# Splitting the first loads over two DMA queues, with fewer weight loads and another work order, in a fused attention and feed-forward kernel

## The chip, the cores and the metric

The kernel runs on one core of a Trainium2 chip. The metric is the device time of one execution in microseconds; lower is better. The five engines of the core are TensorE (PE), VectorE (DVE), ScalarE (ACT), GpSimd (POOL) and SyncE (SP). SyncE, ScalarE and GpSimd can issue DMA transfers, each on a queue of its own.

## The reference

The input is one sequence of 2048 rows with 640 columns, all in bf16. It is normalised row by row, and two branches read the normalised rows `xn`:

```python
x = A_x
xn = _layernorm(x, axis=-1)
return x + _A_ref(xn, A_wqkv, A_wo) + _B_ref(xn, B_w1, B_b1, B_w2, B_b2)

# branch A: 32 heads of 20 columns, each row sees itself and the 7 rows
# at distances 2, 4, ..., 14 before it
off = jnp.arange(8) * 2
logits = einsum("bhsd,bhswd->bhsw", q, k[rows - off]) * 20 ** -0.5   # rows before 0: -1e9
o = einsum("bhsw,bhswd->bhsd", softmax(logits), v[rows - off])
A = o.reshape(B, S, 640) @ wo

# branch B: 640 -> 1536 -> 640
B = gelu(xn @ w1 + b1) @ w2 + b2
```

## The kernel before

The 2048 rows are cut into 16 blocks of 128 and four chunks of 512 rows (`NCH` = 4, `BPC` = 4 blocks each). The chunks are numbered `n` = 0 to 3, and everything runs with features on the partitions: `xnT` is the transposed normalised chunk.

Each chunk goes through the same steps. Statistics of its blocks: `st` on VectorE (two halves and an aggregation, L213 and L215) or, for chunks 2 and 3 and for block 1, sums and squares `su` and `sq` on ScalarE (L225, L232). Then the inverse deviation `rs` (logarithm and exponential on ScalarE, L244 and L247), the normalisation `xn` (L262, L264), and the transpose: on TensorE for chunk 0 (`tp`, L279, copied out by `tc`, L284), by DMA for the others (L291). Then the projections to q, k and v: for chunk 0 in small pieces (`ga`, `gb`, `gd`, `ge` for q of blocks 0 and 1, L346; `hj` for pairs of blocks, L377), for the others as groups of five 512-column matmuls (`pj`, L333), each copied out of PSUM by ScalarE (`gc`, `hc`, `pc`). The attention products of q with k are VectorE work (`qk`, L430), folded over the feature tiles (`pa`, L465, and `pb`, L471), summed per head by TensorE (`lg`, the logits, L480), then a softmax (`cp`, `m`, `mx`, `ex`, `ss`, `ri`, `at`). The weights of the softmax are spread over partitions by DMA (`xe`), multiplied with v (`av`, L581), and folded (`ac`, on VectorE or by an accumulating DMA, `ad`, `ot`). The feed-forward branch is `f1` (five matmuls, L611) and `ge` (gelu on ScalarE, L627). The output product takes w2 and wo: `t` for chunks 0 to 2 (three or five matmuls, L690), turned by `u`, `ut` and added to the output in memory by `ud`; `o` and `ohi` for the last chunk (L646), added to x by `dl` and `dh` (L658) and stored (L663). The output first receives x itself (`xp`, L300).

The order in which all these pieces are issued is written out by hand in `ORDER` (L40): each engine runs its own pieces strictly in that order and waits on semaphores for what others deliver. Ahead of the list stand the input loads, in the order of the queues, and a filling of matmuls on a constant: `WARM` of 512 columns and three of 128.

The first loads: SyncE issues block 0 of x, q's weights, blocks 2 and 3, k's weights, blocks 4 to 7, v's weights and w1 in two halves (L126, L129, L142). ScalarE issues block 1 and the two biases (L132 to L134). A small memset of block 1's first columns on GpSimd (L120) stands ahead of block 1's load. The biases land as rows in `b_rt`, are turned by one matmul `tb` (L453) and copied to `bT` by `b1` (L456). `ldx`, `ld2` and `ldo` issue the rest of x, w2 and wo on SyncE later (L148, L153, L157).

Of the kernel before, what the change touches and what calls it, by code (L numbers as in the profile page):

```python
# [45 lines left out]
pa01 su20 xp2 pj110 pc100 ld2 pj101 pc110 su22 pb01 pj104 su21 pj102 pc101 su23 pb04 pj114 pc104 ng2 pc102 pj112 ldo
sq22 sq21 lg0 pj111 cp0b cp0a pc112 pj113 mask m0b pc111 pc114 m0a xp1 hj211 pc113 mx0b xp0 mx0a hj210 qk13 ex0a pj122
ex0b hc210 pj123 sq23 ss0b t040 pc122 ss0a sq20 pj124 qk12 hc211 t000 rs2 pc123 f10_4 ri0a pc124 pj120 ri0b at0a rc2
qk11 f10_6 pj121 ge0_4 xn23 f10_7 xn21 qk10 tc23 t041 ge0_6 t001 tc21 pc121 su33 f10_8 pc120 at0b f11_9 su32 pa10 xe00
ge0_7 f11_1 xn20 f11_3 ge0_8 tc20 pa11 xn22 f11_10 ge1_1 tc22 ge1_9 t042 pb11 su31 xe03 t002 xe02 hj202 f10_9 xe01  # L50
hc202 ge1_10 pb14 su30 f10_10 ge0_9 pj203 ge0_10 lg1 pc203 pj210 cp1a av00 cp1b f11_5 ng3 sq32 f11_0 pc210 ge1_5 av01
pj202 ac00 ge1_0 hj212 pc202 pj212 sq30 m1 hc212 pj211 ac01 ge1_3 sq31 av03 t003 pad12 pj222 pc211 pc212 pad21 pj201
mx1 pj220 av02 ex1 t043 pc201 pj224 sq33 pj204 ss1 pc220 pc224 f12_6 pc222 ac03 ri1 pj223 at1 pj214 pc223 ac02 xe10
pc204 pj200 xe13 rs3 pc214 xe12 ad00 pad22 pj213 pc200 xe11 rc3 ad01 f11_6 pc213 xn33 pj221 ot00 xn30 tc33 ot01 f11_8
av10 t004 tc30 t044 u00 t010 av13 u04 ut00 t011 xn32 t012 xn31 tc32 t013 ud00 t014 av11 tc31 ac10 t030 u01 t031 pc221
t032 t033 ac13 ac11 t034 av12 f11_7 t020 t021 ge2_6 t022 ge1_6 ac12 t023 ge1_8 t024 u03 ut01 ad11 f12_9 ot11 pj303
ge2_9 qk22 f11_2 f11_4 ge1_2 pc303 pj301 qk23 ge1_4 f11_11 t130 ge1_11 t131 ad10 ge1_7 f12_2 u02 pc301 ut02 pa21 t140
pad31 ge2_2 pj300 ut03 pj311 ot10 ut04 ud01 f12_3 qk21 pc311 pc300 f13_2 ud02 pj312 xb qk20 pj314 pc312 ud03 pj302
pc314 ge2_3 pj313 pa20 pj304 t132 pc304 pb21 t133 pc302 t134 t141 u13 pb24 f13_5 pj310 ge3_5 ge3_2 lg2 t142 cp2a t143
cp2b t100 pc310 m2 pad32 f13_4 pc313 mx2 t101 qk30 f13_3 ex2 t144 f13_0 ss2 u14 f13_1 qk33 t102 ge3_3 ge3_1 t103 ge3_4  # L60
t110 f13_10 qk31 t104 ri2 f13_8 qk32 ge3_0 pj322 u10 f12_10 ge3_10 t111 at2 ge2_10 f12_8 pa31 pc322 xe22 ut10 f13_6
t112 pa30 f12_5 xe21 xe23 t113 ge2_5 xe20 t120 pb31 ge3_8 f12_0 ge3_6 ge2_8 t114 pb34 f12_4 u11 ut11 ud10 pj321 lg3
pj324 cp3b av21 ge2_4 t121 pc324 t122 cp3a pj323 m3 ac21 f12_7 pc323 mx3 ge2_0 t123 ge2_7 av20 o300 pc321 f13_9 f12_1
ex3 av23 ac20 f13_11 t124 ge2_1 pj320 ac23 u12 ge3_9 ut12 ud11 ud04 f13_7 pc320 ss3 ge3_11 t200 ge3_7 t230 av22 t231
f12_11 ri3 o301 at3 o302 ac22 xe33 ge2_11 t201 xe32 t202 xe31 ad21 t203 ut13 o320 ot21 t232 ad20 o310 o311 ut14 ot20
o312 av33 t204 t233 u20 t234 ut20 av32 t210 u23 ud12 xe30 t211 t212 t213 av31 t220 t221 t214 t222 ac31 u21 t223 t224
av30 t240 u22 ud13 ud20 ut21 ud14 t241 t242 t243 ac30 o330 t244 ac32 o321 u24 ud21 ut22 ad30 ud22 ut23 o331 ut24 o313
ot30 o322 ac33 o303 ud23 o304 ad31 o314 ud24 ot31 dh0 o323 dh1 dl1 o324 dl0 dd1 dd0 o332 dl2 o333 dh2 dd2 o334 ohi dl3
dlo dh3 dhi
# [4 lines left out]
def kernel(  # L74
# [47 lines left out]
    wqkv_v = A_wqkv.rearrange("(t p) n -> p t n", p=P)
    w1_v = B_w1.rearrange("(t p) n -> p t n", p=P)

    def load_x(b0, b1):
        nc.sync.dma_start(x_sb[:, b0:b1, :], x_nb[:, b0:b1, :])  # L126

    def load_w(s):
        nc.sync.dma_start(wqkv[s][:], wqkv_v[:, :, s * D : (s + 1) * D])  # L129
# [2 lines left out]
    nc.scalar.dma_start(x_sb[:, 1, :], x_nb[:, 1, :])  # L132
# [4 lines left out]
    load_w(1)
    load_x(BPC, 2 * BPC)
    load_w(2)
    for c in range(2):  # L140
# [1 line left out]
        nc.sync.dma_start(w1_sb[:, :, cs], w1_v[:, :, cs])  # L142
# [5 lines left out]

    def do_ld2():
        w2_v = B_w2.rearrange("(t p) n -> p t n", p=P)  # L150
        for c in range(4):
# [1 line left out]
            nc.sync.dma_start(w2_sb[:, ts, :], w2_v[:, ts, :])  # L153
# [286 lines left out]
    def do_warm(n, cols):  # L440

        for _ in range(n):
            nc.tensor.matmul(
                idle[:, 0:cols],
                lhsT=ones[:, 0:P],
                rhs=ones[:, 0:cols],
                start=True,
                stop=True,
            )
# [3 lines left out]
        nc.tensor.matmul(tiles["tb"][:, 0 : FT + KT], lhsT=b_rt[:], rhs=ident[:, 0 : FT + KT], start=True, stop=True)  # L453

    def do_b1():
        nc.vector.tensor_copy(bT[:], tiles["tb"][:, 0 : FT + KT])  # L456
# [394 lines left out]
```

## Time and profile before

| | us |
|---|---|
| median of 3 runs | 205.5 (205.43 to 206.93) |
| the profiled execution, device time | 205.49 |
| its span, first to last instruction | 203.3 |
| TensorE busy | 199.4 (98%) |
| VectorE busy | 185.8 (91%) |
| ScalarE busy | 129.7 (64%) |
| GpSimd busy | 29.5 (14%) |

All times in the views are microseconds from the start of the span. A row of the timeline gives start, length, engine, source line, operation, what is written from what, shapes and count, and in brackets how long the engine stood before and what released it. Rows with a `q` behind the engine (SPq, ACTq) are DMA issues by that engine. In the view by stretches each row gives, per engine, the busy time and in brackets the count of instructions, then the TensorE clock, the mean busy share of the DMA engines and the rate in GB/s.

### The profile page before, as it was taken

The page shows a single profiled execution, that of the slowest core. Times are in us where ns is not written, and L with a number is a line of the kernel's source. Part 1 is how long each engine was busy: PE and PEld are TensorE (multiplying, and loading weights), DVE is VectorE, ACT ScalarE, POOL GpSimd, SP SyncE. Part 2 cuts the span into 40 slices and gives each one's busy share as a digit, 9 for nine tenths or more (in the row PEclk, how much of TensorE's full clock was granted, in tenths as well). Part 3 has the DMA queues.
Part 4 walks back from the last instruction along what each step waited for, and adds up shares of the span by engine and source line. Part 5 has one row for each costly group of instructions (what it writes and reads, how often), then busy time and mean ns, then how long its engine had stood idle before and what let it go on. Part 6 is the DMA issues. An engine that isn't in the chain of part 4 may idle for free.

```text
span 203.3 us, 2874 instructions
## 1 busy us (share of the span) xinstructions
PE 199.4 (98%) x1100; PEld 105.0 (52%) x1100; DVE 185.8 (91%) x159; ACT 129.7 (64%) x237; POOL 29.5 (14%) x35
## 2 busy tenths in 40 slices
PE   8999999999999999999999999999999999999994
PEld 3899455654454555444444544444444445444552
DVE  2899999899997999999999996999979999999981
ACT  5689979999979897555545437697447990211100
POOL 3000000000000400024202500000202702253420
PEclk9999999999999999999999999999999999999999
DMA  6996399940673681849912890001863898895951
GB/s 204 390 395 208 77 355 336 348 148 3 91 155 89 110 148 22 219 92 163 193 17 52 102 99 5 3 0 15 170 98 69 153 118 147 111 120 90 103 90 64
DMA packets 38430, 27.31 MB, mean 134 GB/s; under 512 B 25106, under 2 KB 34578, under 8 KB 38418
## 3 DMA queue, kind: packets, MB, share of 16 engines
q1 hardware_dynamic: 28016, 20.29, 38.2%
q0 software_dynamic: 10080, 6.56, 26.3%
q10 hardware_dynamic: 322, 0.30, 0.4%
q8 instruction: 8, 0.13, 0.3%
q14 instruction: 4, 0.03, 0.0%
HBM read 10.49 MB, written 4.59 MB: 74 GB/s over the span
## 4 chain that ended last, share of the span: by engine, by line
PE 96%; DMA 2%; SPq 0%; DVE 0%; issue 0%
PE T L690 27%; PE hps L611 25%; PE pps L333 24%; PE lo L646 7%; PE gps L377 7%; DMA wq_sb<-in_A_wqkv_dram 2%; PE hi L646 2%; PE gps L346 1%; PE L L480 1%; PE tp L279 0%; SPq L126 0%; DVE prod L658 0%; PE tb L453 0%
## 5 line engine op out<-in xcount | busy, mean ns | idle before, releaser
L611 PE MATMUL hps<-xnT,w_sb 128*128 128x512 bf16 x240 | 56.9, 379 | 0.0
L430 DVE TENSOR_TENSOR prod<-qT,kT 128x5120 bf16<-128x5120 bf16 x16 | 44.5, 2820 | 0.1
L690 PE MATMUL T<-hT,w_sb 128*128 128x512 bf16 x180 | 43.4, 379 | 0.0
L611 PEld LDWEIGHTS <-w_sb 128*128 128x128 bf16 x240 | 23.5, 98 | 27.5
L702 POOL DMA_DIRECT2D out_dram<-x_sb x15 | 20.9, 1492 | 87.5 <-DMA x_sb<-x_sb 87.5
L627 ACT ACTIVATE hT<-hps,bT 128x512 bf16<-128x512 f32 x36 | 23.9, 689 | 12.1 <-PE hps L611 9.6
L690 PEld LDWEIGHTS <-w_sb 128*128 128x128 bf16 x180 | 17.5, 98 | 21.1 <-issue 0.4
L693 ACT ACTIVATE x_sb<-T,bT 128x512 bf16<-128x512 f32 x15 | 10.3, 688 | 25.6 <-PE T L690 24.5
L581 DVE TENSOR_TENSOR prod<-vT,ax 128x5120 bf16<-128x5120 bf16 x8 | 22.4, 2820 | 2.7 <-PE L L480 1.5
L581 DVE TENSOR_TENSOR prod<-vT,x_sb 128x5120 bf16<-128x5120 bf16 x8 | 22.2, 2817 | 0.0
L592 POOL DMA_DIRECT2D prod<-prod x6 | 7.8, 1300 | 77.5 <-DVE prod L581 77.5
L170 ACT ACT_TABLE_LOAD x14 | 18.0, 1283 | 1.0 <-PEq L835 0.7
L471 DVE TENSOR_TENSOR prod<-prod 128x4096 bf16<-128x4096 bf16 x8 | 18.3, 2291 | 0.3
L333 PE MATMUL pps<-xnT,wv_sb 128*128 128x512 bf16 x75 | 18.5, 379 | 0.0
L690 PE MATMUL T<-oT,wo 128*128 128x512 bf16 x75 | 18.5, 379 | 0.0
L333 PE MATMUL pps<-xnT,wq_sb 128*128 128x512 bf16 x75 | 18.1, 379 | 0.0
L465 DVE TENSOR_TENSOR prod<-prod 128x4096 bf16<-128x4096 bf16 x8 | 18.0, 2286 | 0.0
L333 PE MATMUL pps<-xnT,wk_sb 128*128 128x512 bf16 x75 | 18.0, 380 | 0.0
L594 DVE TENSOR_TENSOR prod<-prod 128x2560 bf16<-128x2560 bf16 x10 | 14.8, 1487 | 0.1
L333 PEld LDWEIGHTS <-wq_sb 128*128 128x128 bf16 x75 | 8.8, 117 | 7.5
L333 PEld LDWEIGHTS <-wv_sb 128*128 128x128 bf16 x75 | 8.7, 118 | 7.6 <-issue 0.4
L333 PEld LDWEIGHTS <-wk_sb 128*128 128x128 bf16 x75 | 8.6, 118 | 7.7 <-issue 0.8
(91 smaller groups left out, 242.6 us busy)
## 6 DMA issues: line engine op xcount, KB each, us to landing
prod<-prod POOLq DMA_DIRECT2D x6, 640.0 KB, 6.8
ax<-attn SPq DMA_DIRECT2D x8, 256.0 KB, 3.9
x_sb<-attn SPq DMA_DIRECT2D x8, 256.0 KB, 4.5
w_sb<-in_B_w_dram SPq DMA_DIRECT2D x2, 960.0 KB, 11.0
out_dram<-x_sb SPq DMA_DIRECT2D x3, 640.0 KB, 6.8
w_sb<-in_B_w_dram SPq DMA_DIRECT2D x4, 480.0 KB, 6.6
out_dram<-x_sb POOLq DMA_DIRECT2D x15, 128.0 KB, 5.6
x_sb<-in_A_x_dram SPq DMA_DIRECT2D x2, 640.0 KB, 7.0
```

Source lines behind the costliest of these rows:

```text
L170: nc.scalar.preload_act_table_set(name)
L333: nc.tensor.matmul(ps[:], lhsT=wqkv_p[which][:, ti, to, :], rhs=xnT[:, ti, :], start=(ti == 0), stop=(ti == KT - 1),)
L430: nc.vector.tensor_tensor(out=prod[:, j], in0=q[:, :, at].unsqueeze(1).to_broadcast([P, W, KT, P]), in1=window(k, at), op=ALU.mult,)
L465: nc.vector.tensor_tensor(out=low, in0=low, in1=high, op=ALU.add)
L471: nc.vector.tensor_tensor(out=first, in0=first, in1=rows[:, :, t * P : (t + 1) * P], op=ALU.add)
L581: nc.vector.tensor_tensor(out=prod[:, j], in0=window(qkv_tile(n, 2), slice(j * P, (j + 1) * P)), in1=ax_view(n)[:, j, :, :].unsqueeze(2).t ...
L594: nc.vector.tensor_tensor(out=low, in0=low, in1=high, op=ALU.add)
L611: nc.tensor.matmul(ps[:], lhsT=w1_sb[:, ti, ft * P : (ft + 1) * P], rhs=tiles["xnT", n][:, ti, :], start=(ti == 0), stop=(ti == KT - 1),)
L627: nc.scalar.activation(hT, tiles["hps", n, ft][:], ACT.Gelu_apprx_tanh, bias=bT[:, ft : ft + 1], scale=1.0)
L646: nc.tensor.matmul(out_ps(bl, hi), lhsT=lhs, rhs=rhs[:, CH:D] if hi else rhs[:, 0:CH], start=pc == 0 and k == 0, stop=pc == 4 and k == len ...
L690: nc.tensor.matmul(ps[:], lhsT=lhs, rhs=rhs, start=pc == 0 and k == 0, stop=pc == 4 and k == len(srcs) - 1)
L702: nc.gpsimd.dma_start(dst, src, accum_op=ALU.add)
```

## The change

- Blocks 0 and 1 of x are each loaded as two halves of 64 partitions, the first half on SyncE's queue and the second on ScalarE's. q's weights are loaded in two parts as well: feature tiles 0 to 2 by SyncE, 3 and 4 by ScalarE. The memset ahead of block 1 is gone.
- The biases are loaded by SyncE, behind v's weights and ahead of w1. `bT` is copied by ScalarE and no longer by VectorE.
- w1 is one load instead of two, w2 three instead of four, wo two instead of three.
- The filling has 9 long matmuls instead of 10.
- `ORDER` is another permutation of the same pieces.

```diff
-WARM = 10
+WARM = 9
...
-    nc.gpsimd.memset(x_sb[:, 1, 0:16], 0.0)
...
-    load_x(0, 1)
-    nc.scalar.dma_start(x_sb[:, 1, :], x_nb[:, 1, :])
-    nc.scalar.dma_start(b_rt[0:FT, :], B_b1.rearrange("(t p) -> t p", p=P))
-    nc.scalar.dma_start(b_rt[FT : FT + KT, :], B_b2.rearrange("(t p) -> t p", p=P))
-    load_w(0)
+    for b in range(2):
+        for queue, ps in ((nc.sync, slice(0, P // 2)), (nc.scalar, slice(P // 2, P))):
+            queue.dma_start(x_sb[ps, b, :], x_nb[ps, b, :])
+    for queue, a, b in ((nc.sync, 0, 3), (nc.scalar, 3, KT)):
+        queue.dma_start(wqkv[0][:, a:b, :], wqkv_v[:, a:b, 0:D])
     load_x(2, BPC)
     load_w(1)
     load_x(BPC, 2 * BPC)
     load_w(2)
-    for c in range(2):
-        cs = slice(c * F // 2, (c + 1) * F // 2)
-        nc.sync.dma_start(w1_sb[:, :, cs], w1_v[:, :, cs])
+    nc.sync.dma_start(b_rt[0:FT, :], B_b1.rearrange("(t p) -> t p", p=P))
+    nc.sync.dma_start(b_rt[FT : FT + KT, :], B_b2.rearrange("(t p) -> t p", p=P))
+    nc.sync.dma_start(w1_sb[:], w1_v)
...
-        for c in range(4):
-            ts = slice(c * FT // 4, (c + 1) * FT // 4)
+        for c in range(3):
+            ts = slice(c * FT // 3, (c + 1) * FT // 3)
             nc.sync.dma_start(w2_sb[:, ts, :], w2_v[:, ts, :])
...
-        for a, b in COLS:
+        for a, b in ((0, 3), (3, KT)):
             nc.sync.dma_start(wo2[:, a:b], A_wo.rearrange("(p t) n -> p t n", t=KT)[:, a:b])
...
-        nc.vector.tensor_copy(bT[:], tiles["tb"][:, 0 : FT + KT])
+        nc.scalar.copy(bT[:], tiles["tb"][:, 0 : FT + KT])
```

The two orders begin like this (of 626 names each):

```diff
-pad01 pad02 st00a st00 sum1 rs00 neg1 xn00a sq1 xn00b tp00a wa tp00b tc00a wb rs01 tc00b ga xn01b gb2 xn01a tp01b
-st03a tp01a tb tc01b gb3 tc01a gb4 st03 gd gc0 st02a ge rs03 st02 hj101 xn03 rs02 gc1 xn02 tp03 gc4 st12a tp02 tc03
+pad02 pad01 st00a st00 sum1 rs00 neg1 xn00a sq1 wa xn00b tp00a ho tp00b tc00a wb ga tc00b rs01 gb2 xn01a xn01b tp01a
+gb3 st03a tp01b tc01a gb4 st02a tc01b gd st02 gc0 ge st03 rs02 hj101 xn02 rs03 gc1 xn03 tp02 gc4 tp03 st10a hj100 tc03
```

Further differences that the prediction speaks of: `ho`, the reduce that makes `head_of` (L190), moves from behind the statistics of chunk 1 to between `tp00a` and `tp00b`; `tb` and `b1` move to behind k's and q's pieces of chunk 0; `xp1` takes the place of `xp2` behind `ldx`, ahead of `ld2`; on VectorE `qk32` moves ahead of `m2`; around the fourth logits `lg3` three `f1` groups (`f12_0`, `f12_8`, `f13_0`) move behind it and `t121`, `t122`, `t123` ahead of it.

More of the change, by code (lines that the diff above doesn't have):

```diff
@@ L46 @@
[L46 to L69, printed above, removed]
+pad02 pad01 st00a st00 sum1 rs00 neg1 xn00a sq1 wa xn00b tp00a ho tp00b tc00a wb ga tc00b rs01 gb2 xn01a xn01b tp01a
+gb3 st03a tp01b tc01a gb4 st02a tc01b gd st02 gc0 ge st03 rs02 hj101 xn02 rs03 gc1 xn03 tp02 gc4 tp03 st10a hj100 tc03
@@ new lines @@
+sq23 hj202 ss0a pj120 hc202 pc121 ss0b ri0a hj211 sq20 qk10 hj210 pc120 ri0b pc122 pj123 rs2 hc210 f10_4 rc2 qk12 xn21
+f10_9 hc211 tc21 pc123 f10_8 qk11 f10_6 ge0_4 xn22 f10_10 ge0_9 tc22 t041 ge0_10 pa11 f11_1 pad21 ge0_6 xn20 f10_7
+ge0_8 pa10 tc20 f11_10 xn23 ge0_7 t001 tc23 su33 f11_3 at0a at0b ge1_10 pb11 xe00 t002 ge1_1 xe03 f11_9 xe02 pj124
+ge1_9 pb14 xp2 su32 hj212 pc124 pj203 xe01 ge1_3 su31 lg1 pj213 su30 av00 cp1a f11_0 hc212 ng3 pc203 pj210 sq32 av02
+pad12 pj214 ac00 ge1_0 pc210 pj201 cp1b pc213 pc214 f11_5 av01 sq30 t042 ge1_5 pj211 sq31 t043 sq33 m1 ac01 pj212 mx1
@@ new lines @@
+pj224 av03 rs3 pc201 t003 pc212 pj221 ex1 pj204 pc211 ss1 pj202 pc204 ac02 ri1 pj200 pc202 pc221 at1 pj223 rc3 ac03
+xe11 xn30 pj220 xe12 pc200 xe10 ad00 pc224 f11_8 xn33 xe13 pj222 pc223 ad01 pc220 tc30 f11_4 ot00 f11_6 ot01 av11 t004
+tc33 t044 u00 pc222 t010 u04 ut00 av12 ac11 t011 xn31 t020 xn32 tc31 t021 t022 av10 t023 tc32 t012 t013 f11_7 av13
+ac10 t014 t024 ud00 u01 pad31 t030 ac13 t031 ge1_6 t032 ac12 ge1_4 t033 t034 ad11 f11_2 u03 ut01 ge1_7 ot11 f12_2
+ge1_2 qk23 f11_11 ge2_2 pad22 f12_6 ge1_11 ge1_8 f12_3 qk22 ge2_6 pj314 pj303 ad10 t130 pc303 pj300 ot10 pj312 pc300
@@ new lines @@
+pa21 pc314 t131 u02 pj313 ge2_3 ut02 pc312 qk21 f13_5 pc313 ut03 t132 ut04 ud01 pj311 qk20 pj304 pc311 ud02 t140 pc304
+pj301 ud03 pa20 pj302 xb pj310 pc302 pb21 t133 f13_2 t134 ge3_2 pb24 pc310 f12_9 ge3_5 pc301 t141 u13 lg2 f12_4 cp2a
+qk32 cp2b t100 ge2_9 pj322 t142 m2 f13_1 mx2 t101 qk33 ex2 t143 t102 t144 ge2_4 qk31 f13_8 ge3_1 f13_4 ge3_8 u14 f13_6
+pc322 ss2 t120 f12_5 qk30 ri2 f13_10 t121 ge2_5 t122 at2 ge3_4 t103 pa31 ge3_10 xe21 f13_3 xe22 xe20 t104 ge3_3 pa30
+pj321 u10 ut10 t110 t111 pb31 t112 xe23 t113 t114 pb34 f12_10 u11 ut11 ud10 t123 lg3 f12_1 av20 t124 ge2_1 cp3a pj320
@@ new lines @@
+pc321 cp3b av21 f12_7 ac20 ge2_10 ge3_6 f12_11 u12 pad32 pc320 ut12 pj324 ge2_7 av23 ac21 f13_0 ud11 f12_0 ge3_0
+ge2_11 ud04 m3 f13_9 ge2_0 mx3 pj323 ac23 f12_8 ex3 t230 ss3 o300 ge3_9 t231 av22 ge2_8 t200 t201 t232 ri3 f13_7 at3
+o301 ac22 xe30 ge3_7 t202 xe31 pc323 t233 xe33 ad20 pc324 t203 ut13 o310 ot20 o311 ad21 f13_11 ot21 ut14 o312 av30
+t204 t234 u20 ut20 t210 u23 ud12 ac30 t211 xe32 t212 av31 t213 t220 t221 t222 t214 av33 t223 u21 t224 t240 ac31 u22
+ud13 ud20 ut21 ud14 t241 ge3_11 t242 ad30 t243 o302 ac33 t244 av32 o320 u24 ud21 ut22 o303 ud22 ut23 ut24 o321 o322
@@ L70 @@
+ac32 o330 o331 ot30 ud23 o313 ad31 o323 ud24 o304 ot31 o314 dh0 dl0 dd0 o324 dl1 dh1 dd1 o332 dh2 dl2 o333 dd2 o334
+ohi dl3 dlo dh3 dhi
 """.split()
```

8 lines of the change are left out of this document (5 added, 3 removed).

## The prediction

> **What bounds the kernel now.** I read the page first, then the chain of work that ended last in order of time, then the waits, then the first 36 us instruction by instruction.
>
> ```profile
> span 203.3 us, 2874 instructions
> ...
> PE 199.4 (98%) x1100; PEld 105.0 (52%) x1100; DVE 185.8 (91%) x159; ACT 129.7 (64%) x237; POOL 29.5 (14%) x35
> ...
> PE 96%; DMA 2%; SPq 0%; DVE 0%; issue 0%
> ```
>
> The chain of work in order of time (start, length, what):
>
> ```profile
> 1.19 5.07 DMA wq_sb<-in_A_wqkv_dram
> 6.31 1.03 PE gps L346 x15
> ...
> 9.64 1.09 PE gps L377 x10
> 10.73 0.56 PE tp L279 x10
> ...
> 43.05 0.65 PE T L690 x3
> ...
> 45.42 1.08 PE hps L611 x5
> ...
> 200.62 0.29 DVE prod L658
> ```
>
> From 6.31 to 200.6 us the chain is TensorE and nothing else: a group of five 512-column matmuls costs 1.08 us and a group of three 0.65 us wherever it stands, so 194.3 us of the span is matmul work laid end to end. The change neither removes nor adds any matmul behind 6.31. A new order can therefore only keep this stretch or put holes in it; a gain must come from ahead of 6.31, and it must survive the next meeting of TensorE with another engine. So I looked at the front, engine by engine:
>
> ```profile
> 0.74 0.39 SPq L126 DMA_DIRECT2D x_sb<-in_A_x_dram  x1
> ...
> 0.88 0.38 ACTq L132 DMA_DIRECT2D x_sb<-in_A_x_dram  x1
> ...
> 3.27 0.89 DVE L213 BATCH_NORM_STATS2 stats<-x_sb 128x6 f32<-128x320 bf16 x2 [3.27 <-DMA x_sb<-in_A_x_dram]
> ...
> 3.65 0.74 ACT L225 ACTIVATE trash<-x_sb 128x640 bf16<-128x640 bf16 x1 [1.63 <-DMA x_sb<-in_A_x_dram]
> ...
> 4.50 0.29 ACT L244 ACTIVATE logv<-mv,eps_t 128x1 f32<-128x1 f32 x1
> ```
>
> ```profile
> PEld L346 <- DMA wq_sb<-in_A_wqkv_dram: 0.3, 1, 0.3
> ```
>
> Block 0 lands at 3.27, block 1 at 3.65, q's weights at 6.3. The first q matmul needs the first copy of block 0's transpose and the weights; the weights come last, and TensorE stands 0.3 us for them. Next, the meeting at the first logits (L480):
>
> ```profile
> 10.88 1.28 DVE L213 BATCH_NORM_STATS2 stats<-x_sb 128x6 f32<-128x320 bf16 x3 [0.22 <-DMA x_sb<-in_A_x_dram]
> ...
> 14.90 0.23 DVE L190 TENSOR_REDUCE head_of<-ident 128x32 bf16<-128x128 bf16 x1
> 15.05 0.17 DVE L456 COPY bT<-tb 128x17 f32<-128x17 f32 x1
> ...
> 15.66 11.03 DVE L430 TENSOR_TENSOR prod<-qT,kT 128x5120 bf16<-128x5120 bf16 x4
> ...
> 31.13 4.62 DVE L471 TENSOR_TENSOR prod<-prod 128x4096 bf16<-128x4096 bf16 x2
> ```
>
> ```profile
> 33.44 2.32 PE L333 MATMUL pps<-xnT,wk_sb 128*128 128x512 bf16 x10
> 35.80 0.62 PE L480 MATMUL L<-prod,head_of 128*32 128x512 bf16 x8
> ```
>
> VectorE's last fold ends at 31.13 + 4.62 = 35.75 and the logits start at 35.80. TensorE was through with its ten matmuls at 33.44 + 2 x 1.08 = 35.60, so it already stands some 0.1 to 0.2 us for VectorE. And VectorE has no gap from 15.66 to 35.75; that run begins where it does because blocks 4 to 7 of x landed at 10.88. Whoever wants the end earlier must bring those blocks earlier as well as TensorE's start.
>
> **The change part by part.**
>
> *Blocks 0 and 1 and q's weights over two queues.* The bytes in front of blocks 4 to 7 stay the same, but for the 4 KB of biases. What can be won is fill of the DMA engines:
>
> ```profile
> 2.50:3.00 0.50, 0.50 (x3) 0.22 (x2) 0.00 (x0) 0.00 (x0) 0.00 (x0) 1.00 1.08 359
> 3.00:3.50 0.50, 0.50 (x3) 0.17 (x2) 0.23 (x1) 0.00 (x0) 0.00 (x0) 1.00 0.93 261
> 3.50:4.00 0.50, 0.50 (x2) 0.15 (x1) 0.50 (x2) 0.35 (x1) 0.00 (x0) 1.00 0.88 318
> ...
> 4.50:5.00 0.50, 0.50 (x5) 0.28 (x3) 0.00 (x0) 0.47 (x3) 0.00 (x0) 1.00 1.08 397
> ```
>
> The last column is GB/s. Between 3.0 and 4.0 it is 261 and 318 against 397 later: (397 - 261) x 0.5 + (397 - 318) x 0.5 = 107 KB not moved, or 0.27 us at 397 GB/s. That is the most that a second queue can win for everything loaded behind it. The loss from the other side: each queue now issues two loads, not one, ahead of q's weights, and SyncE's issues stand 0.45 us apart (0.74 and 1.19), so the weights may start 0.45 us later. I take a gain of 0.13 us, half of the most, since both halves of the weights then have a queue that is already running. The trace has no split load, hence the bounds +0.27 and -0.45.
>
> The chain from block 0 to the first q matmul: the logarithm at 4.50 stands behind block 1's sum on ScalarE (3.65 + 0.74 and 0.19 more to read it), so block 0 alone being earlier brings nothing; block 1 has to be earlier too. The two blocks are the same bytes as before on the same two queues, and ScalarE's first issue no longer waits for the small memset (0.88 back to 0.74): 0 to 0.14 us. The weights' wait of 0.3 us bounds it too. TensorE's start moves by 0 to -0.3 us; I take -0.13 as well.
>
> [...]
>
> *The reduce of `head_of` moves from 14.90 to between the two normalisations and the first transposed copy.* It takes 0.23 us where VectorE waits for the transposes anyway, so I charge 0.05 us; without that cover 0.23. At 14.90 it hid, as did the bias copy (0.17, now on ScalarE), behind ScalarE's step for the inverse deviations: VectorE was through at 15.05 + 0.17 = 15.22 and its next large product began at 15.66. So their removal there gives nothing.
>
> *Biases behind v's weights.*
>
> ```profile
> wv_sb<-in_A_wqkv_dram SPq DMA_DIRECT2D x1, 800.0 KB, 9.3
> ```
>
> ```profile
> 3.65 0.85 SPq L129 DMA_DIRECT2D wv_sb<-in_A_wqkv_dram  x1
> ```
>
> v's weights land at 3.65 + 9.3 = 12.95, and the biases right behind. The matmul that turns them now stands behind five pieces of 1.09, one of 0.55 and ten transposes of 0.56 after the first k piece at 9.5, so at about 16.0: cover of 3 us. Behind it on TensorE stand all later matmuls, so lateness would be paid in full. Cost 0.
>
> *w1 in one load.* Its second half went out at about 6.7 and landed 12.0 us later, at 18.7:
>
> ```profile
> L142 SPq DMA_DIRECT2D w_sb<-in_B_w_dram x2: 368/1092/1816, 6.3 to 6.7; - x2
> ...
> DMA to landing us min/median/max: 6.3/8.5/12.0
> ```
>
> The first feed-forward matmul is at 20.5, and now needs all of w1: cover of 1.8 us, cost 0. w2 in three loads and wo in two save issues on SyncE, and the store of x that stands before them now copies blocks 4 to 7, long landed, and no longer blocks of the load just issued.
>
> ```profile
> 28.27 3.12 SPq L153 DMA_DIRECT2D w_sb<-in_B_w_dram  x4
> ```
>
> ```profile
> w_sb<-in_B_w_dram SPq DMA_DIRECT2D x4, 480.0 KB, 6.6
> ```
>
> The last of w2 was issued by 31.4 and landed some 6.6 us later, at 38.0. Its first use, 43 now, comes behind the first logits and four groups of five: 35.80 + 0.62 + 4 x 1.08 = 40.7. Even the old issue times leave 2.7 us. Cost 0.
>
> *One warm-up matmul fewer.*
>
> ```profile
> 0.78 4.43 PE L443 MATMUL idle<-const-bfloat16-1.0 128*128 128x512 bf16 x13 [0.78 <-PEq L835]
> ```
>
> ```profile
> 2.01 0.15 PEld L443 LDWEIGHTS <-const-bfloat16-1.0 128*128 128x128 bf16 x1 [0.28 <-issue]
> 2.44 0.15 PEld L443 LDWEIGHTS <-const-bfloat16-1.0 128*128 128x128 bf16 x1 [0.28 <-issue]
> ...
> 4.57 0.46 PEld L443 LDWEIGHTS <-const-bfloat16-1.0 128*128 128x128 bf16 x3 [0.28 <-issue]
> ```
>
> They start 0.43 us apart, twice the 0.216 us of later ones; from 4.57 on three loads fit in 0.46 us, so full speed comes some 3.9 us after the start. Nine of 0.43 and three short ones end at about 4.9, just past it. TensorE does nothing useful then: 0 us, with a rival below.
>
> *The other order.* I added up TensorE's groups ahead of each meeting in both orders. Ahead of the first and the third logits stand the very same pieces; ahead of the second one group of three is replaced by five short matmuls (0.1 us earlier). Ahead of the fourth, three groups of five give way to three groups of three: 3 x (1.08 - 0.65) = 1.3 us earlier. There VectorE's slack was less:
>
> ```profile
> 144.84 4.62 DVE L471 TENSOR_TENSOR prod<-prod 128x4096 bf16<-128x4096 bf16 x2
> ```
>
> ```profile
> 150.29 0.62 PE L480 MATMUL L<-prod,head_of 128*32 128x512 bf16 x8
> ```
>
> ```profile
> 125.73 0.43 DVE L524 TENSOR_TENSOR attn<-e 128x512 bf16<-128x512 bf16 x1 [1.82 <-ACT e L517]
> ```
>
> 150.29 - 149.46 = 0.83, so TensorE would stand 0.5 us. But VectorE's wait of 1.82 us at 125.7 is now filled by a product of q and k (`qk32` ahead of `m2`), and the fold ends up to 1.8 us earlier. Net cost 0, and 0.5 if that product's inputs are late. The last two meetings (the output's last five-tile sums) stand behind the same pieces on both engines. The tail is the same.
>
> **The sum.** 205.49 (the profiled execution, whose span is 203.3; 2.2 lie around it, and the median of the runs is 205.50) - 0.13 = 205.36, with the bounds of the split from 205.49 - 0.27 - 0.1 (TensorE's stand at the logits) = 205.1 to 205.49 + 0.45 = 205.9. **Forecast 205.4 us: no change that can be told apart.**
>
> **The rivals.**
>
> *The halves come late* (slower). ScalarE's queue carries half of block 0, and what it issued at 0.88 landed 0.38 us after SyncE's load. If each block waits for that queue and q's weights start a whole issue later, blocks 4 to 7 and TensorE's start both move by 0.45: 205.9. For it: the two landings; against it: that load was a whole block, not a half.
>
> *The split moves nothing*: the engines are shared, both orders hold, 205.5. For it: 1.08 of DMA share already at 2.5 us.
>
> *The clock is released late* (slower than before). Nine warm-ups end 0.2 us past the release seen here. If a release later than about 4.9 is missed and the count starts again with the transposes near 5.3, full speed comes at 5.3 + 3.9 = 9.2, and the q matmuls from 6.3 on run at half: (9.2 - 6.3) / 2 = 1.45, so 206.9. It decides from the point where the release falls behind the filling. Against it: the fast executions agree. [...]
>
> *A hole in the new order* (slower). One VectorE product, 11.03 / 4 = 2.8 us, ahead of its turn at a meeting without slack would be paid in full: 205.4 + 2.8 = 208.2. For it: TensorE has no slack anywhere; against it: the sums above.
>
> **How the numbers follow.** Forecast 0.62, halves late 0.15, nothing moves 0.10, late clock 0.07, hole 0.06. A measurement of this kernel tells about 1% (2.05 us) from no change. Only the hole goes beyond that: slower 0.06. No case gains 2 us, since the whole wait for the weights is 0.3: faster 0.01. The rest, 0.93, is the same. The range reaches from 205.0, under the best bound, to 207.0, over the late clock.
>
> **What would show it.** Right: the first q matmul at 6.1 to 6.3, VectorE's statistics of block 4 at 10.7 to 10.9, the first logits at 35.6 to 35.8, the last matmul near 200.5, and no TensorE wait over 0.3 us between. Wrong: q's weights after 6.5, half-speed rows behind 6.3, TensorE waiting at the fourth logits, or the bias matmul waiting for its load.

## The result and the profile after

| | before | after |
|---|---|---|
| median of the runs, us | 205.48 (205.22 to 208.37, 9 runs) | 207.18 (206.32 to 208.0, 9 runs) |
| ratio | | 1.0077, interval 1.0049 to 1.0104 |
| profiled execution, us | 205.49 | 206.32 |
| its span, us | 203.3 | 204.2 |

Here and below, medians and ranges count every run, while ratios and their 95% intervals leave out the few executions over 1.5% slower than the fastest of their kernel. The changed kernel is slower by 1.7 us in the median and by 0.8 us in its profiled execution, which is the fastest of its nine. The interval lies clear of 1, although the change is smaller than the 1% that the prediction took for the least that can be told. So there are two things to find: what every execution pays, and what most of the others pay on top. The head of the page of after and the shares of its chain:

```profile
PE 199.3 (98%) x1099; PEld 105.0 (51%) x1099; DVE 185.8 (91%) x158; ACT 129.1 (63%) x238; POOL 29.4 (14%) x34
...
PE 81%; DVE 12%; DMA 4%; SPq 1%; issue 0%; ACT 0%
```

TensorE has the same 199 us of work. But the chain, 96% TensorE before, now holds 12% VectorE and 4% DMA. In order of time (start, length, what) it begins like this:

```profile
0.74 0.60 SPq L132
...
1.40 0.80 SPq L132
...
2.25 0.61 SPq L134
...
2.91 0.49 SPq L125
...
3.95 7.77 DMA x_sb<-in_A_x_dram
...
16.62 10.94 DVE prod L430 x4
27.56 4.41 DVE prod L465 x2
...
34.32 2.30 DVE prod L471
...
36.67 0.61 PE L L480 x8
```

This is the changed place itself: SyncE's issues of the two halves (0.60 and 0.80 us) and of q's part (0.61) push the issue of blocks 4 to 7 to 3.95; they land at 11.72; from there to 36.62 the chain is VectorE, but for half a microsecond of ScalarE's inverse deviations, and the first logits wait for it. The timeline of after has the times to set beside those of the prediction:

```profile
0.74 1.47 SPq L132 DMA_DIRECT2D x_sb<-in_A_x_dram  x2
0.74 1.20 ACTq L132 DMA_DIRECT2D x_sb<-in_A_x_dram  x2
1.97 0.60 ACTq L134 DMA_DIRECT2D wq_sb<-in_A_wqkv_dram  x1
...
3.36 0.89 DVE L213 BATCH_NORM_STATS2 stats<-x_sb 128x6 f32<-128x320 bf16 x2 [3.36 <-DMA x_sb<-in_A_x_dram]
...
4.69 0.74 ACT L225 ACTIVATE trash<-x_sb 128x640 bf16<-128x640 bf16 x1 [0.80 <-DMA x_sb<-in_A_x_dram]
...
6.37 0.63 PE L279 MATMUL tp<-ident,xn 128*128 128x128 bf16 x5 [1.17 <-DVE xn L264]
...
7.05 1.00 PE L346 MATMUL gps<-xnT,wq_sb 128*128 128x128 bf16 x15
...
11.74 1.67 DVE L213 BATCH_NORM_STATS2 stats<-x_sb 128x6 f32<-128x320 bf16 x4 [0.24 <-DMA x_sb<-in_A_x_dram]
...
36.67 0.61 PE L480 MATMUL L<-prod,head_of 128*32 128x512 bf16 x8 [0.18 <-DVE prod L471]
```

Block 0 is there at 3.36 (3.27 before), block 1 at 4.69 (3.65), the first q matmul at 7.05 (6.31), blocks 4 to 7 at 11.74 (10.88), the first logits at 36.67 (35.80). TensorE stands 1.17 us between the filling and the first transposes. The first logits are 0.87 us later and the last long stretch of the output product 0.85 us (198.11 against 197.26), which is the whole difference of the spans (204.2 against 203.3, each rounded to a tenth). TensorE itself was ready for the logits at 36.67 - 0.18 = 36.49, 0.69 us later than they began before. So both ways to the logits became late, and VectorE's a little more.

Where the 0.86 us of the loads went is in the view by stretches, the first 5 us and the next 5 of before and then of after (last column GB/s):

```profile
0.00:5.00 5.00, 4.22 (x13) 1.62 (x13) 1.10 (x3) 2.58 (x6) 1.53 (x13) 1.00 0.62 202
5.00:10.00 5.00, 4.64 (x73) 4.15 (x71) 4.46 (x14) 3.33 (x12) 0.00 (x0) 1.00 1.06 389
```

```profile
0.00:5.00 5.00, 4.22 (x13) 1.68 (x13) 1.10 (x3) 1.60 (x2) 1.49 (x12) 1.00 0.51 129
5.00:10.00 5.00, 3.83 (x60) 3.30 (x59) 3.77 (x13) 3.50 (x12) 0.00 (x0) 1.00 1.06 385
```

In 5 us after moved (202 - 129) x 5 = 365 KB less, and 20 KB less in the next five. At 389 GB/s that is 0.99 us of lateness for whatever stands behind. The prediction read the split as a way to fill the DMA engines; with it they moved less. They were emptier on the mean (busy share 0.51 against 0.62), but not all the time:

```profile
3.00:3.50 0.50, 0.50 (x3) 0.16 (x2) 0.14 (x1) 0.50 (x1) 0.00 (x0) 1.00 1.16 156
```

In this half microsecond of after the DMA engines are busy throughout and move 156 GB/s, where before moved 261 at a share of 0.93. Late issues are therefore not all of it, and what makes the moving itself slow is not settled.

### The profile page after: what moved, and what is told of

The parts are those of the page before. It is cut to its first block, busy times and chain, and to the rows that moved or that the text cites. A ratio compares the mean times of both kernels' runs of the same rounds, so it can differ in the third digit from the quotient of the medians.

```text
span 204.2 us, 2875 instructions
## 1 busy us (share of the span) xinstructions
PE 199.3 (98%) x1099; PEld 105.0 (51%) x1099; DVE 185.8 (91%) x158; ACT 129.1 (63%) x238; POOL 29.4 (14%) x34
## 4 chain that ended last, share of the span: by engine, by line
PE 81%; DVE 12%; DMA 4%; SPq 1%; issue 0%; ACT 0%
PE T L690 27%; PE hps L611 22%; PE pps L333 20%; PE lo L646 7%; DVE prod L430 5%; DMA x_sb<-in_A_x_dram 4%; DVE prod L471 2%; DVE prod L465 2%; PE hi L646 2%; PE gps L377 2%; DVE stats L213 2%; PE L L480 1%; SPq L132 1%; DVE mv L215 0%; SPq L134 0%
## 5 line engine op out<-in xcount | busy, mean ns | idle before, releaser
L611 PE MATMUL hps<-xnT,w_sb 128*128 128x512 bf16 x240 | 56.1, 379 | 0.0
L702 POOL DMA_DIRECT2D out_dram<-x_sb x15 | 20.3, 1575 | 68.3 <-DMA x_sb<-x_sb 68.0
L592 POOL DMA_DIRECT2D prod<-prod x6 | 7.3, 1212 | 95.6 <-DVE prod L581 91.2
L397 ACT CAST qT<-pps 128x512 bf16<-128x512 f32 x15 | 8.7, 585 | 7.1 <-PE pps L333 7.0
## 6 DMA issues: line engine op xcount, KB each, us to landing
w_sb<-in_B_w_dram SPq DMA_DIRECT2D x1, 1920.0 KB, 12.2
```

The source lines that it names most:

```text
L611: nc.tensor.matmul(ps[:], lhsT=w1_sb[:, ti, ft * P : (ft + 1) * P], rhs=tiles["xnT", n][:, ti, :], start=(ti == 0), stop=(ti == KT - 1),)
L702: nc.gpsimd.dma_start(dst, src, accum_op=ALU.add)
```

## The experiments

The theories. *Split*: the halves of blocks 0 and 1 and the parts of q's weights are slow to issue and slow to move, and delay blocks 4 to 7, hence the first logits. *Clock*: with less filling and a longer stand behind it, TensorE loses its full clock in some executions. *Order*: something in the new order, the biases, w1, w2 or wo costs. `WARM` is the number of long warm-up matmuls.

### More filling: e1_warm12

```diff
-WARM = 9
+WARM = 12
```

> The changed kernel with 12 long warm-up matmuls instead of 9; nothing else. Theory of the late clock (part of the loss, in most runs, is TensorE at half speed behind its longer stand before the first transposes): the median falls from 207.2 to 206.3-206.6, near the profiled execution of the changed kernel, and the runs lie closer together. Rival (the clock has no part; all of it is the late loads): 207.2 as before, block 1 of x still at 4.7.

Measured: 206.46 (206.17 to 207.0, 12 runs), ratio 1.0040, interval 1.0020 to 1.0059. Blocks 4 to 7 are there at 11.88 and the logits come at 36.80, as late as in after. So some 1.0 us of the loss stays with a longer filling, and 0.7 us of the median goes; the two intervals still overlap, so the 0.7 is rough. Three of after's nine runs had a mean granted clock of 0.990 to 0.992; none of these twelve is below 0.998. The experiments that follow bear this out: of all runs with halves by partitions and 9 or 10 long warm-ups (after, e3, e4, e7, e8), 19 of 47 have a mean clock of 0.992 or less, of those with the first loads whole and 9 or 10 (before, e2, e6) 5 of 99, of e5, where block 1 stands behind a part of q's weights, three of four, and of those with 12 (e1, e9 to e12) none of 44.

Why a longer filling helps is not shown. When full speed comes is seen in the filling's weight loads: they stand 0.43 us apart at half speed and close up with full speed, from 4.57 in before (shown above), and in e1 and then in e12, which is the kernel before with 12, from

```profile
3.72 1.35 PEld L443 LDWEIGHTS <-const-bfloat16-1.0 128*128 128x128 bf16 x8 [0.28 <-issue]
```

```profile
5.82 0.16 PEld L443 LDWEIGHTS <-const-bfloat16-1.0 128*128 128x128 bf16 x2 [0.24 <-issue]
```

So the moment of full speed lies 2.1 us apart in these executions (3.72 and 5.82), which the prediction could not see in one trace, and a filling that ends near 5 us (5.20 in after, none of it at full speed) ends ahead of it in some.

### Before's first loads in the changed kernel: e2_old_first_loads

```diff
-    for b in range(2):
-        for queue, ps in ((nc.sync, slice(0, P // 2)), (nc.scalar, slice(P // 2, P))):
-            queue.dma_start(x_sb[ps, b, :], x_nb[ps, b, :])
-    for queue, a, b in ((nc.sync, 0, 3), (nc.scalar, 3, KT)):
-        queue.dma_start(wqkv[0][:, a:b, :], wqkv_v[:, a:b, 0:D])
+    load_x(0, 1)
+    nc.scalar.dma_start(x_sb[:, 1, :], x_nb[:, 1, :])
+    load_w(0)
```

The small memset is back too; all else is as changed, `WARM` 9 included.

> The changed kernel with the loads of blocks 0 and 1 and of q's weights as they were before (block 0 and q whole on SyncE, block 1 whole on ScalarE behind the small memset); the other loads, the order, the 9 warm-ups stay changed. Theory of the split (two queues that issue at once hold each other up, block 1 and then blocks 4 to 7 come 0.9 late): block 1 at 3.6, blocks 4 to 7 at 10.8-10.9, the first logits at 35.8, 205.3-205.7. Rival (the order or the later biases or the whole w1 cost): 206 or more with the early landings back.

Measured: 205.72 (205.34 to 208.96, 12 runs), ratio 1.0005, interval 0.9986 to 1.0024. The rows of its timeline:

```profile
0.74 0.40 SPq L126 DMA_DIRECT2D x_sb<-in_A_x_dram  x1
...
1.20 0.41 SPq L129 DMA_DIRECT2D wq_sb<-in_A_wqkv_dram  x1
...
6.31 1.00 PE L345 MATMUL gps<-xnT,wq_sb 128*128 128x128 bf16 x15
...
35.86 0.62 PE L479 MATMUL L<-prod,head_of 128*32 128x512 bf16 x8
```

The first q matmul is back at 6.31 and the logits at 35.86. The loss hangs on the first loads; order, biases, w1, w2, wo and one warm-up fewer cost nothing here that can be told apart (the interval leaves room for up to 0.5 us).

### The split alone, in the kernel before: e3_split_alone

```diff
-    load_x(0, 1)
-    nc.scalar.dma_start(x_sb[:, 1, :], x_nb[:, 1, :])
-    load_w(0)
+    for b in range(2):
+        for queue, ps in ((nc.sync, slice(0, P // 2)), (nc.scalar, slice(P // 2, P))):
+            queue.dma_start(x_sb[ps, b, :], x_nb[ps, b, :])
+    for queue, a, b in ((nc.sync, 0, 3), (nc.scalar, 3, KT)):
+        queue.dma_start(wqkv[0][:, a:b, :], wqkv_v[:, a:b, 0:D])
```

> The kernel before with only the split: blocks 0 and 1 in halves and q's weights in two parts over both queues, no memset ahead of block 1; old order, 10 warm-ups, biases on ScalarE. Theory of the split: blocks 4 to 7 land at 11.6-11.8, 206.3-207.2. Rival (the order): 205.5.

Measured: 207.21 (206.86 to 208.35, 7 runs), ratio 1.0083, interval 1.0054 to 1.0111: as much as the whole loss, from the split alone (the memset that goes with it is tested in e6). Its profiled execution (208.35) is one of two that lost the clock by the mean (0.989 and 0.990). The other five, at 1.000, still took 206.86 to 207.62, more than late loads of some 1.0 us explain, and no trace of them is kept. TensorE's rows, and then the view by stretches, whose third figure from the right is the granted clock:

```profile
6.62 0.29 PE L280 MATMUL tp<-ident,xn 128*128 128x128 bf16 x2 [1.60 <-DVE xn L265]
...
7.37 1.50 PE L347 MATMUL gps<-xnT,wq_sb 128*128 128x128 bf16 x15
```

```profile
7.00:8.00 1.00, 0.99 (x14) 0.82 (x14) 0.77 (x3) 0.72 (x4) 0.00 (x0) 0.88 1.03 378
8.00:9.00 1.00, 1.00 (x13) 1.00 (x11) 0.86 (x3) 0.00 (x0) 0.00 (x0) 0.50 1.07 397
9.00:10.00 1.00, 1.00 (x13) 1.00 (x12) 0.57 (x2) 0.48 (x1) 0.00 (x0) 0.50 1.07 396
10.00:11.00 1.00, 1.00 (x12) 1.00 (x11) 0.97 (x4) 0.58 (x2) 0.00 (x0) 0.50 1.06 394
11.00:12.00 1.00, 1.00 (x20) 1.00 (x18) 0.81 (x4) 0.87 (x5) 0.00 (x0) 0.92 1.06 392
```

TensorE had stood 1.60 us behind the filling, ran the transposes and the first q matmuls at full speed (nine in 0.86 us), and was then at half: a share of 0.12 / 0.5 = 0.24 of the slice to 8, three whole slices, and 0.08 / 0.5 = 0.16 of the one to 12, 3.4 us in all. That costs 3.4 / 2 = 1.7 us, and 1.7 / 206 = 0.8% is about what a mean clock of 0.990 to 0.992 lacks. The full clock was not given late here; it was taken back after a stand. The profiled executions of e4, e5 and e7 also read 0.50 in the slices from 9 to 11, behind stands of 1.24, 2.45 and 1.77 us. How much standing costs the clock, and what sets the length of the stretch, is not shown.

Part of that stand may not be the loads. In e3 ScalarE still issues the biases, so the load of its tables comes behind five issues, and block 1's sum begins only when that load ends:

```profile
3.63 1.28 ACT L171 ACT_TABLE_LOAD   x1 [3.63 <-DMA x_sb<-in_A_x_dram]
...
4.93 0.74 ACT L226 ACTIVATE trash<-x_sb 128x640 bf16<-128x640 bf16 x1
```

### q's weights whole, the blocks in halves: e4_q_whole

```diff
-    for queue, a, b in ((nc.sync, 0, 3), (nc.scalar, 3, KT)):
-        queue.dma_start(wqkv[0][:, a:b, :], wqkv_v[:, a:b, 0:D])
+    load_w(0)
```

> The changed kernel with q's weights whole on SyncE; x still in halves. If the four half loads alone do the harm: block 1 still at 4.5-4.7, 206.3-207.2. If the fifth and sixth issue of q's parts do it: block 1 at 3.6-3.8, 205.4-205.8.

Measured: 208.05 (206.45 to 210.4, 11 runs), ratio 1.0096, interval 1.0069 to 1.0123, above what was expected. In its profile block 1 is there at 4.23, earlier than in after and between the two expectations, but q's weights, in one piece behind two half loads, come late:

```profile
7.90 1.32 PE L345 MATMUL gps<-xnT,wq_sb 128*128 128x128 bf16 x13 [1.24 <-DMA wq_sb<-in_A_wqkv_dram]
```

Seven of the eleven runs show a mean clock of 0.992 or less. So with halves ahead it looks better to split q's weights too, though the intervals of the two kernels overlap. The halves do harm without the parts of q. That a longer stand costs the clock more often fits (seven of eleven against three of nine in after) but is not shown by so few runs.

### The blocks whole, q in parts: e5_x_whole, and again as e9_q_split_only

```diff
-    for b in range(2):
-        for queue, ps in ((nc.sync, slice(0, P // 2)), (nc.scalar, slice(P // 2, P))):
-            queue.dma_start(x_sb[ps, b, :], x_nb[ps, b, :])
+    load_x(0, 1)
+    nc.scalar.dma_start(x_sb[:, 1, :], x_nb[:, 1, :])
```

> The changed kernel with block 0 whole on SyncE and block 1 whole on ScalarE behind the small memset, as before; q's weights still in two parts over both queues. Theory (the four half loads of x are the harm, not the split of q): block 1 at 3.6-3.9, blocks 4 to 7 at 10.7-10.9, 205.4-205.8. Rival (every load beside another queue's is slowed, so q's split costs as well): blocks 4 to 7 at 11.2 or later, 206.0 or more.

Measured: 208.94 (208.76 to 209.81, 4 runs), ratio 1.0143, interval 1.0061 to 1.0224. It was not the edit that was meant. With the memset kept, ScalarE's part of q's weights went out first, at 0.74, and block 1 behind it at 1.24; block 1 landed at 5.85 instead of 3.65, and TensorE stood 2.45 us. It says nothing on the parts of q, only that the order on the second queue counts in microseconds. The clean form has no memset and `WARM` 12:

> The changed kernel with 12 long warm-ups, blocks 0 and 1 whole (block 0 on SyncE, block 1 on ScalarE), q's weights in two parts as changed. If the halves of x are what is slow to issue: block issues of 0.39 to 0.41 us, block 1 lands by 3.9, blocks 4 to 7 at 10.9 to 11.1, first logits at 35.8 to 36.0, 205.4 to 205.8. If each further load ahead costs, whatever its shape: q's parts issue in 0.6 us each, blocks 4 to 7 near 11.3, 206.0.

Measured: 206.03 (205.7 to 206.8, 8 runs), ratio 1.0031, interval 1.0018 to 1.0043. Its issues and its first 10 us by stretches:

```profile
0.74 0.40 SPq L125 DMA_DIRECT2D x_sb<-in_A_x_dram  x1
0.74 0.40 ACTq L131 DMA_DIRECT2D x_sb<-in_A_x_dram  x1
...
1.18 0.47 ACTq L133 DMA_DIRECT2D wq_sb<-in_A_wqkv_dram  x1
1.20 0.42 SPq L133 DMA_DIRECT2D wq_sb<-in_A_wqkv_dram  x1
```

```profile
0.00:5.00 5.00, 4.22 (x11) 1.52 (x12) 1.09 (x3) 2.18 (x4) 1.48 (x12) 1.00 0.61 207
```

With whole blocks ahead, the same parts of q's weights take 0.42 and 0.47 us to issue and not 0.60; the rate is 207 GB/s, blocks 4 to 7 are there by 10.93, the logits at 35.94. The front is as the first expectation has it, and the parts of q cost next to nothing there. The time is not: it stands 0.6 us over before, at the rival's 206.0; what is left of it stands in e11.

### The memset: e6_no_memset

```diff
-    nc.gpsimd.memset(x_sb[:, 1, 0:16], 0.0)
```

In the kernel before, so that both queues issue a whole block at 0.74.

> The kernel before without the small memset that stands ahead of block 1's load, so that both queues issue at 0.74 at once, whole blocks. Theory that two issues at the same moment hold each other up: both take 0.55-0.6 instead of 0.39, block 0 lands 0.2-0.4 later, and the load of ScalarE's tables starts behind its three issues at 2.4 instead of 0.74; time 205.6-206.2. Rival (only half loads are slow): issues of 0.39 as before, 205.4-205.5.

Measured: 205.52 (205.32 to 208.08, 10 runs), ratio 0.9997, interval 0.9961 to 1.0033. Both issues take 0.39 to 0.41 us. So the idea that two issues at the same moment hold each other up falls: it is the halves that are slow to issue. The landing is another matter:

```profile
3.73 0.89 DVE L212 BATCH_NORM_STATS2 stats<-x_sb 128x6 f32<-128x320 bf16 x2 [3.73 <-DMA x_sb<-in_A_x_dram]
```

Block 0 is there at 3.73 and in e9, also without the memset, at 3.70, against 3.27 in before; the first logits of e6 come at 36.07, 0.27 us later. Two profiles suggest that a block which starts together with another lands later, as the theory had it, but the median shows no price.

### A memset ahead of ScalarE's half: e7_split_behind_memset

```diff
+    nc.gpsimd.memset(x_sb[P // 2 :, 0, 0:16], 0.0)
```

> The changed kernel with a small memset ahead of ScalarE's first half load, as it stood ahead of block 1 before; all four halves and both parts of q as changed. If the simultaneous first issue does most of the harm: issues of 0.4, block 1 at 3.8-4.0, 205.6-206.2. If the half loads themselves do it (more loads, later queue): block 1 still at 4.5-4.7, blocks 4 to 7 at 11.6-11.8, 206.3-207.2.

Measured: 207.72 (206.3 to 209.19, 10 runs), ratio 1.0080, interval 1.0041 to 1.0120. It did not stagger the queues: ScalarE sent block 1's half first, at 0.74, and block 0 was complete only at 4.70. The halves were as slow to issue as in after (two in 1.20 us on ScalarE, two in 1.48 on SyncE), and blocks 4 to 7 came at 12.31. Since the first two issues still fell together, it does not separate the theories.

### All halves on one queue: e8_one_queue

```diff
-        for queue, ps in ((nc.sync, slice(0, P // 2)), (nc.scalar, slice(P // 2, P))):
+        for queue, ps in ((nc.sync, slice(0, P // 2)), (nc.sync, slice(P // 2, P))):
...
-    for queue, a, b in ((nc.sync, 0, 3), (nc.scalar, 3, KT)):
+    for queue, a, b in ((nc.sync, 0, 3), (nc.sync, 3, KT)):
```

> The changed kernel with all four halves and both parts of q on SyncE's queue; ScalarE issues none of them. No two queues issue together here, so if the meeting of two queues is the harm, each issue takes 0.39-0.45 and four stand ahead of q: block 1 at 4.0-4.3, blocks 4 to 7 at 11.0-11.3, 205.8-206.5. If half loads are slow by themselves: issues of 0.6-0.8, block 1 beyond 4.6, 206.5 or more.

Measured: 208.01 (207.56 to 208.66, 10 runs), ratio 1.0086, interval 1.0062 to 1.0110.

```profile
0.74 2.52 SPq L132 DMA_DIRECT2D x_sb<-in_A_x_dram  x4
3.30 1.12 SPq L134 DMA_DIRECT2D wq_sb<-in_A_wqkv_dram  x2
...
13.21 1.67 DVE L213 BATCH_NORM_STATS2 stats<-x_sb 128x6 f32<-128x320 bf16 x4 [0.45 <-DMA x_sb<-in_A_x_dram]
...
38.13 0.61 PE L480 MATMUL L<-prod,head_of 128*32 128x512 bf16 x8
```

Four halves take 2.52 us to issue with no other queue issuing, 0.63 each against 0.40 for a whole block; 72 GB/s in the first 5 us; blocks 4 to 7 and the logits 2.33 us later than before. SyncE issues blocks 4 to 7 at 5.49, 2.75 us later than before, where after was 1.21 later: the suspected cost is more than doubled, and so is the lateness of the logits.

This profile holds something else. TensorE's matmuls are at half speed from its first transposes on, though the granted clock reads 1.00:

```profile
8.00:9.00 1.00, 1.00 (x12) 1.00 (x11) 0.62 (x2) 0.00 (x0) 0.00 (x0) 1.00 0.98 296
```

```profile
7.70 1.79 PE L346 MATMUL gps<-xnT,wq_sb 128*128 128x128 bf16 x15
```

15 q matmuls take 1.79 us here and 1.00 in after; at 10.26 the next thirty run in 1.84. The filling had run at half speed to its end (13 matmuls in 4.43 us), TensorE then stood 1.58 us, and half speed went on to about 10.1; the mean granted clock (1.00) shows nothing of it. The missed release of the prediction's rival would look like this, but that it is one is not shown: after's filling, too, ran at half speed to its end (13 matmuls in 4.42 us; the four short ones take 311 ns on the mean against 221 for three in before), and yet its transposes at 6.37 and its q matmuls were at full speed behind a stand of 1.17 us.

### Halves by columns: e10_column_halves

```diff
-        for queue, ps in ((nc.sync, slice(0, P // 2)), (nc.scalar, slice(P // 2, P))):
-            queue.dma_start(x_sb[ps, b, :], x_nb[ps, b, :])
+        for queue, cs in ((nc.sync, slice(0, D // 2)), (nc.scalar, slice(D // 2, D))):
+            queue.dma_start(x_sb[:, b, cs], x_nb[:, b, cs])
```

`WARM` is 12.

> The changed kernel with 12 long warm-ups, blocks 0 and 1 halved by columns (128 partitions of 320 columns) and not by partitions, over the same two queues; q's weights in two parts. If 64 partitions make a load slow to issue: issues of about 0.4 us, block 1 lands by 4.1, blocks 4 to 7 near 11.0, 205.5 to 205.8. If it is the number of loads, issues stay at 0.6 us, blocks 4 to 7 at 11.7 to 11.9, 206.4 as with partition halves and 12 warm-ups.

Measured: 206.97 (206.62 to 207.28, 4 runs), ratio 1.0074, interval 1.0059 to 1.0089.

```profile
0.74 0.87 SPq L132 DMA_DIRECT2D x_sb<-in_A_x_dram  x2
0.74 0.89 ACTq L132 DMA_DIRECT2D x_sb<-in_A_x_dram  x2
...
12.05 1.28 DVE L213 BATCH_NORM_STATS2 stats<-x_sb 128x6 f32<-128x320 bf16 x3 [0.39 <-DMA x_sb<-in_A_x_dram]
```

The issues bear out the first theory: of two loads of the same 80 KB, the one with 128 partitions takes 0.44 us to issue, the one with 64 partitions 0.60 and more (after). The landing (12.05) and the time fit neither: both are worse than either theory had them, and the first 5 us still move only 158 GB/s. So the slow issue is not the whole cause; a block in two pieces loses either way.

### Twelve warm-ups without the split: e11_old_loads_warm12 and e12_before_warm12

e11 is e2 with `WARM` 12, e12 the kernel before with `WARM` 12.

> All of the change but its first loads (blocks 0 and 1 and q's weights as before, memset kept), with 12 long warm-ups. If order, biases, w1, w2 and wo cost nothing and the clock does the rest: 205.3 to 205.6. If the new order has a small price of its own that the earlier run with 9 warm-ups hid in its scatter: 205.8 or more.

Measured: 205.95 (205.48 to 208.23, 10 runs), ratio 1.0029, interval 0.9998 to 1.0059.

> The kernel before with 12 long warm-ups in place of 10, nothing else. If the clock is only lost where TensorE stands over 1 us behind the warm-ups, 205.3 to 205.5, equal to before with fewer runs above 206. If the longer filling is itself in the way of the first transposes (5.6), they start 0.2 to 0.4 us later and the time is 205.6 to 205.9.

Measured: 205.50 (205.23 to 206.82, 10 runs), ratio 1.0014, interval 0.9998 to 1.0030. Neither beats the kernel before, which had 205.39 on that chip. e11's median falls on the side of its second expectation, but its interval reaches down to no change: the rest of the change may cost half a microsecond, or nothing (e2), and which is left open. e9 stands level with e11, so the parts of q add nothing to it. In e12 two of ten runs are above 206, against one of 23 of before, so the longer filling did not make long runs rarer there.

Both profiled executions are the slowest of their ten, and they hold a delay that is neither the split nor the clock. With before's first loads and matmuls at full speed, q's weights came at 8.76 in e11 and 7.69 in e12, and blocks 4 to 7 at 13.32 and 12.24. Against before, every load from q's weights to v's took 2.1 to 2.5 us longer from issue to landing in e11 and 1.3 to 1.5 in e12, though nearly as many bytes were moved. Why is not settled, and how many of after's long runs hold the same is not known.

The lateness of the front in one table. The third column is what the missing bytes of the first 10 us make of it: 5 us times the rates lost against before's 202 and 389 GB/s, over 389.

| kernel | GB/s to 5 us, 5 to 10 us | missing bytes, us | first logits against 35.80, us |
|---|---|---|---|
| after | 129, 385 | 0.99 | +0.87 |
| e1, more filling | 131, 376 | 1.08 | +1.00 |
| e8, one queue | 72, 333 | 2.39 | +2.33 |
| e10, column halves | 158, 381 | 0.67 | +1.19 |
| e9, whole blocks, q in parts | 207, 390 | -0.08 | +0.14 |
| e2, before's first loads | 206, 387 | -0.03 | +0.06 |
| e6, before without the memset | 202, 392 | -0.04 | +0.27 |
| e11, e2 with 12 warm-ups, slowest run | 186, 383 | 0.28 | +2.44 |
| e12, before with 12 warm-ups, slowest run | 185, 374 | 0.41 | +1.37 |

Left out are e3, e4, e5 and e7, whose granted clock fell to 0.50 ahead of the logits. All but e10 to e12 fall in line within 0.31 us. In e11 and e12 the loads land late with few bytes missing, as said. In e10 another 0.5 us is lost that the bytes don't explain; SyncE's issue of blocks 4 to 7 came at 3.76, 0.6 us after its neighbour had ended, and why was not settled.

## Why the prediction was wrong, step by step

*The step that failed: blocks 0 and 1 and q's weights over two queues.* It was put at a gain of 0.13 us with bounds from +0.27 to -0.45, for blocks 4 to 7 and again for TensorE's start. Measured: blocks 4 to 7 later by 0.86, TensorE's first q matmul by 0.74, block 1 by 1.04. The method of the term (bytes not moved over the rate) holds for after, e1 and e8 in the table; its sign did not. The lower bound took one whole load's issue, 0.45, for the price of a second load on a queue. In truth SyncE issues blocks 4 to 7 at 3.95 instead of 2.74, 1.21 later: two halves at 0.60 and 0.80 in the place of one load of 0.39, and the part of q's weights behind them 0.61 in the place of 0.42. What makes 64 partitions slow to issue, and halves slow to move, stays open. "The two blocks are the same bytes as before on the same two queues" held for the bytes and not for the issues. The rival *the halves come late* had the mechanism, both places and the sign, with half the size: 205.9 stood there, 206.46 was measured in e1, none of whose runs has a low mean clock.

The rival *the split moves nothing* (205.5) put the split's price at nothing; the runs show that it loses 0.87 us of the front.

*One warm-up matmul fewer* was put at nothing, and the late clock at 0.07. Nine against twelve is worth some 0.7 us in the median of the changed kernel, 0.2 the other way and within the scatter with before's first loads (205.72 against 205.95). So it is not the one warm-up by itself (e3 lost the clock with ten): the split lets TensorE stand 1.17 us (after) to 1.60 (e3) behind the filling, where it stood 0.26 before, and with a short filling and the halves together 19 of 47 runs have a low mean clock, with a short filling and the first loads whole 5 of 99, with 12 warm-ups none of 44. Without its three runs of low mean clock after has a median of 206.80, about half of the way to e1's 206.46. The rival *the clock is released late* put 1.45 us and half speed until 9.2 on a missed release, its author's supposition; no run shows one, though e8 has half speed until about 10.1. It did not name what e3 shows, the clock taken back, worth 1.7. "The fast executions agree" spoke for a kernel that hardly stood there. The prediction also took nine long and three short matmuls to end just past the release; in after's profile none of the filling is at full speed. How many of after's runs lost the clock, and how, is not shown: after's own profile is at full speed from its transposes on, three of nine runs have a low mean clock, and half speed as in e8 leaves no mark in that mean (1.00).

*What was right.* The dependency: "whoever wants the end earlier must bring those blocks earlier", since VectorE has no gap from their landing to the first logits. Landing +0.86, logits +0.87, span +0.9. *The order* made no hole that a profile shows: behind its start TensorE waits in after only those 1.17 us and the 0.18 us at the first logits. Its price, with that of the moved reduce of `head_of`, the biases and the weights, is bounded by e2 and not shown to be nothing (e11). The fourth logits were to come 1.3 us earlier and do:

```profile
149.86 0.62 PE L480 MATMUL L<-prod,head_of 128*32 128x512 bf16 x8
```

150.29 - 1.3 + 0.87 = 149.86. VectorE's wait at 125.7 is 0.82 and no longer 1.82, filled by the product of q and k:

```profile
125.75 2.83 DVE L430 TENSOR_TENSOR prod<-qT,kT 128x5120 bf16<-128x5120 bf16 x1 [0.82 <-PE L L480]
```

*Biases, w1, w2, wo*: no wait of TensorE on them. The bias matmul stands at 16.8, and w1, issued at 7.60 with 12.2 us to landing, was there at 19.8, 1.4 us ahead of its first use at 21.22; the prediction had 1.8. These covers held.

Two of the four signs that were to show it wrong did: SyncE's part of q's weights, issued at 2.25 with 4.7 us to landing, was there at 6.95, after 6.5; and there are half-speed rows behind 6.3, not in after's own profile but in those of e3, e4, e5, e7 and e8. TensorE did not wait at the fourth logits, nor the bias matmul for its load.

## What to carry to other kernels

A load that is cut in two has more than its bytes: count each issue on its queue, and what the queue sends next, and look at whether the bytes in flight fall in the time that follows; here halves for two blocks cost 0.87 us of a span in which TensorE has next to no slack. A wait that looks hidden behind warm-up work need not be free when it grows: in e3 a stand of 1.60 us was followed by half speed that cost another 1.7 us. And a part of a change that is put at "a little gain" deserves the bound from the other side first, with the price of each issue taken as unknown when the shape of the load is new.

## What the runs showed of the hardware

- Among the first two loads of a queue, one of 64 partitions took 0.60 to 0.80 us to issue, also with no other queue issuing (0.63), one of 128 partitions at its head 0.37 to 0.41, one of 128 partitions with half the columns 0.44. The load behind the halves was slow too: q's weights in one piece 0.60 behind halves (e4), 0.42 behind a whole block; the parts of q 0.60 and 0.61 (0.56 in e8) against 0.42 and 0.47. Why is not settled.
- In the profiled execution of e3 TensorE's granted clock fell from 1.00 to 0.50 for one stretch of 3.4 us, which began some 1.1 us behind the end of a stand of 1.60 us; in that of e11, the slowest of its runs, a stand of 2.88 us for q's weights was followed by full speed (15 matmuls in 1.03 us). How long a stand is too long isn't settled by these runs:

```profile
8.76 1.03 PE L345 MATMUL gps<-xnT,wq_sb 128*128 128x128 bf16 x15 [2.88 <-DMA wq_sb<-in_A_wqkv_dram]
```

- The granted clock read 1.00 while matmuls ran at half speed, in the filling of before (weight loads 0.43 us apart, later ones 1.08 / 5 = 0.216) and behind the stand of e8 (15 matmuls in 1.79 us, in after 1.00): the spacing of the matmuls has to be read beside it.
